# Loading a 1 KB row as 16 transfers of 15 down to 1 and 8 chunks, and another as one transfer of 128 chunks

## The chip, the cores and the metric

The kernel runs on one core of a Trainium2 chip. The metric is the device time of one execution in microseconds (us). Three executions of the kernel before took 666.84, 666.91 and 667.05 us; the median is 666.91 us.

## What is computed

Two decode attention blocks, A and B, with inputs of the same shapes, are computed one after the other and their outputs are put side by side. Each has one token x of 512 numbers, 32 heads of width 128, and a cache of 8192 keys and values for each head. All inputs are bf16. Cut to what matters, one block is:

```python
q = (x @ wq).reshape(B, Sq, H, Dh).transpose(0, 2, 1, 3)        # x: 1 x 1 x 512
scores = einsum("bhqd,bhkd->bhqk", q, k_cache) * (Dh ** -0.5)   # k_cache: 1 x 32 x 8192 x 128
p = softmax(scores, axis=-1)
o = einsum("bhqk,bhkd->bhqd", p, v_cache)
out = o.transpose(0, 2, 1, 3).reshape(B, Sq, H * Dh) @ wo
```

x is 1 KB in each block; the four caches are 64 MB each, and the four weight matrices 4 MB each.

## The kernel before

**Tiling.** The 64 heads of A and B are handled four at a time, in 16 rounds, the "quads". A quad's keys and its values are 8 MB each, laid out over 128 partitions with 32 partitions for each head and 256 positions in each partition, so that a partition holds 64 KB of either. Keys have two buffers (`kn`, two slots used in turn), values have one (`vn`).

**One quad.** VectorE multiplies the keys by the broadcast query in four pieces (`plan_mul`, L338), TensorE sums the products over the width with an identity matrix (`plan_red`, L347), VectorE finishes the sums (L358), the maxima and exponentials follow, and TensorE multiplies the probabilities with the values (`plan_pv`, L416). The value product of a quad is done a round later, between the steps of the next quad.

**Start.** The two query weight matrices are loaded into the buffer of the values (`load_wq`, L281), and x of A and of B into the first partition of the second slot of the keys (`xrow`, L193). TensorE spreads each x over the partitions with four matrix products against ones (`xmm`, L298), reading every fourth number of x at a time, since number m·4+c of x belongs to partition m and piece c. ScalarE copies the result to `xb` (L302). Then `plan_q` makes the queries (L316) and ScalarE copies them out (`qbc`, L324). Queries of A are made at the start and those of B inside the first round, between TensorE's third and fourth reduction of the first quad.

**The order of the transfers.** Every transfer is issued by SyncE (SP) through one helper, `dma` (L243), so all of them show that line; the tiles tell them apart. SP's list is in program order: the query weights of A (`load_wq(0)`, L291), x of A, x of B (L292), the keys of the first quad (`load_k(0)`, L497), the query weights of B (`load_wq(1)`, L498), the keys of the second quad, the values of the first quad, and so on in turn. The first five wait for nothing and are issued before the block of all engines starts (L565). The keys of the second quad overwrite the place where x landed, so `load_k` (L271) has them wait for `x_ready`, the second copy of L302. The values of the first quad overwrite the query weights, so `load_v` (L275) has them wait for `q_done[1]`, the last product with the weights of B. Later keys wait for the reduction that read their slot, later values for the value product before. At the end come the output weights (`load_wo`, L284) in pieces, and the last products with them, a 2 KB output and its transfer.

Of the kernel before, what the change touches and what calls it, by code (L numbers as in the profile page):

```python
# [11 lines left out]
P = 128  # L12
# [11 lines left out]
class _Plan:  # L24
# [15 lines left out]
    def op(self, eng, fn, ctr=None, needs=(), inc=1):  # L40

        for m in needs:
            self.wait(eng, m)
        self.prog[eng].append((fn, ctr, inc))
        if ctr is None:
            return None
        ctr.n += inc
        return ctr, ctr.n
# [81 lines left out]
def bass_concat_heads__mha_block_cached__gqa_block_cached__decode_kernel(  # L130
# [13 lines left out]
    xs = [A_x, B_x]  # L144
# [4 lines left out]
    NA = 2  # L149
    H, Sk, Dh = ks[0].shape[1:]  # L150
    D = xs[0].shape[2]
    NOUT = wos[0].shape[1]
    assert Dh == P and H == 32 and D == 512 and NOUT == 512
    C = D // P
# [19 lines left out]
    with ExitStack() as st:  # L174
        ec = st.enter_context

        def sb(name, shape, dt):
            return ec(nc.sbuf_tensor(name, shape, dt))

        kn = sb("kn", [P, NK, T, Dh], BF16)  # L180
        vn = sb("vn", [P, T, Dh], BF16)

        def flat(ap):
            return ap.rearrange("p t d -> p (t d)")
# [5 lines left out]
        KX, KW = 1, (NM - 2) % NK  # L190
        wo_sb = [flat(kn[:, KW])[:, a * W:(a + 1) * W].rearrange("p (j n) -> p j n", n=NOUT)
                 for a in range(NA)]
        xrow = flat(kn[0:1, KX])[:, 0:NA * D].rearrange("p (a d) -> p a d", a=NA)  # L193
        xb = sb("xb", [P, NA, C, P], BF16)
        qbc = sb("qbc", [P, NM, Dh], BF16)
        pt = sb("pt", [P, T, G], BF16)
# [1 line left out]
        ones_bf = sb("ones_bf", [P, P], BF16)  # L198
# [31 lines left out]
        def ctr(name):  # L230
            return _Ctr(nc, st, name)

        s_x = ctr("s_x")
# [8 lines left out]
        def dma(eng, dst, src, c, needs=()):  # L242
            return op(eng, lambda e: e.dma_start(dst, src), c, needs, inc=16)  # L243
# [37 lines left out]
        def load_wq(a):  # L281
            wq_in[a] = dma("SP", wq_buf[a], wqs[a].rearrange("(p c) n -> p (c n)", p=P), s_w[a])
# [6 lines left out]


        load_wq(0)  # L291
        x_in = [dma("SP", xrow[0:1, a, :], xs[a][0], s_x) for a in range(NA)][-1]  # L292

        for a in range(NA):
            def xmm(e, a=a):
                r = None
                for c in range(C):
                    r = e.matmul((misc if a == 0 else qyp)[:, c * P:(c + 1) * P],  # L298
                                 xrow[0:1, a, c:D:C], ones_bf[0:1, :], start=True, stop=True)
                return r  # L300
            m = op("PE", xmm, c_pe, [x_in, i_onesb])
            x_ready = op("ACT", lambda e, a=a: e.copy(  # L302
                xb[:, a].rearrange("p c m -> p (c m)"), (misc if a == 0 else qyp)[:]), c_act, [m])
# [190 lines left out]
        cuts = {n: [] for n in range(L0, L1 + 1)}  # L494
# [151 lines left out]
```

## Time and profile before

| what | value |
|---|---|
| median of three executions | 666.91 us |
| the profiled execution's own time | 666.67 us |
| its span, first to last instruction | 665.4 us |
| TensorE busy | 437.9 us (66%) |
| VectorE busy | 340.1 us (51%) |
| ScalarE busy | 62.4 us (9%) |
| bytes moved | 285.33 MB in 6076 packets |

The span is what the trace covers; the execution's own time is 1.27 us longer, and what lies outside the span is not shown. Busy times are shares of the span. "PE" is TensorE, "PEld" its loading of weights, "DVE" VectorE, "ACT" ScalarE, "SPq" the sequencer of SyncE that issues transfers. In the lists of instructions each line has a start and a length in us, then engine, line of the code, operation and tiles, how often, and in brackets the idle time before it and what ended it. The lines on transfers give packets, bytes and the share of 16 DMA engines that the packets took; where a short stretch is asked for, a packet counts at its start, so that shares above 100% are possible there.

### The profile page before, as it was taken

Reading aid. Unit: us, or ns where it says so; the run is one execution under the profiler, and the core shown is the slowest. Engines: PE = TensorE matmul, PEld = TensorE weight load, DVE = VectorE, ACT = ScalarE, POOL = GpSimd, SP = SyncE. Lnnn points to the kernel's source line nnn. Section 1 sums busy time; section 2 is a strip of 40 time slices with the busy share of each in tenths; the row PEclk is TensorE's granted clock in tenths of the full one; section 3 lists DMA queues with packets and bytes.
Section 4 is the critical chain, followed back from the end, with each engine's and each line's share of the span. In section 5 each row is a group of like instructions: output and inputs, shape, how many; then the busy total and the mean of one; then the engine's idle time right before and its main releaser. Section 6 shows DMA issues by size and latency. Waiting matters only on the chain.

```text
span 665.4 us, 12448 instructions
## 1 busy us (share of the span) xinstructions
PE 437.9 (66%) x5646; PEld 252.7 (38%) x5646; DVE 340.1 (51%) x215; ACT 62.4 (9%) x151; POOL 2.8 (0%) x15
## 2 busy tenths in 40 slices
PE   1164876938388594838759483875948387594865
PEld 0022342616145261614526161442626144262645
DVE  1094908466390736639083563808356381835610
ACT  1002002020200102020110202010020201002020
POOL 1000000000000000000000000000000000000000
PEclk9998857768786676879667687966768787776875
DMA  9999999999999999999999999999999999999997
GB/s 378 439 443 438 438 432 433 414 433 441 429 433 441 441 437 406 437 441 437 425 441 441 433 410 437 441 437 429 437 441 433 414 433 441 437 429 437 410 440 306
DMA packets 6076, 285.33 MB, mean 429 GB/s; under 512 B 690, under 2 KB 948, under 8 KB 1204
## 3 DMA queue, kind: packets, MB, share of 16 engines
q1 hardware_dynamic: 6068, 285.22, 99.3%
q8 instruction: 6, 0.10, 0.1%
q14 instruction: 2, 0.02, 0.0%
HBM read 285.21 MB, written 0.00 MB: 429 GB/s over the span
## 4 chain that ended last, share of the span: by engine, by line
DMA 63%; PE 25%; DVE 10%; issue 2%; SPq 1%; ACT 0%; DVEq 0%
DMA kn<-in_B_k_cache_dram 27%; DMA kn<-in_A_k_cache_dram 18%; PE rps L347 15%; DMA vn<-in_A_v_cache_dram 14%; DVE kn L338 9%; PE acc L416 9%; DMA kn<-in_B_wo_dram 4%; SPq L243 1%; PE qyp L316 0%; DVE s_sb L358 0%; PE misc L400 0%; ACT qbc L324 0%; DVEq L338 0%; PE bmp L486 0%; PE qyp L474 0%
## 5 line engine op out<-in xcount | busy, mean ns | idle before, releaser
L347 PE MATMUL rps<-kn,ident 128*128 128x512 bf16 x1024 | 290.1, 451 | 169.1 <-DVE kn L338 169.1
L338 DVE TENSOR_TENSOR kn<-kn,qbc 128x8192 bf16<-128x8192 bf16 x64 | 281.5, 4419 | 98.2 <-DMA kn<-in_A_k_cache_dram 58.6
L347 PEld LDWEIGHTS rps<-kn,ident 128*128 128x128 bf16 x1024 | 111.5, 113 | 334.7 <-issue 258.0
L416 PE MATMUL acc<-pt,vn 128*128 128x4 bf16 x4096 | 109.4, 166 | 10.8 <-DMA vn<-in_B_v_cache_dram 5.2
L416 PEld LDWEIGHTS acc<-pt,vn 128*128 128x128 bf16 x4096 | 108.5, 101 | 11.6 <-DMA vn<-in_B_v_cache_dram 5.4
L358 DVE TENSOR_REDUCE s_sb<-rps 128x64 f32<-128x512 f32 x64 | 44.0, 687 | 107.4 <-PE rps L347 107.4
L395 ACT ACTIVATE pt<-s_sb,negb 32x256 bf16<-32x256 f32 x64 | 54.8, 857 | 1.9
L387 ACT ACTIVATE negb<-bmp 128x1 f32<-128x1 f32 x16 | 2.7, 171 | 528.8 <-PE bmp L383 528.8
L425 DVE TENSOR_TENSOR oD<-acc,rinv 128x4 f32 (+1 forms) x16 | 2.6, 162 | 97.2 <-PE acc L416 85.1
L383 PE MATMUL bmp<-gm,hrow 1*128 1x1 f32 x128 | 17.8, 256 | 6.0 <-DVE gm L373 6.0
L383 PEld LDWEIGHTS bmp<-gm,hrow 1*128 1x128 f32 x128 | 16.5, 197 | 10.7 <-DVE gm L373 10.0
L370 PE MATMUL mtp<-ident_f,m 128*1 128x128 f32 x32 | 6.1, 271 | 19.8 <-DVE m L364 19.8
L395 ACT ACTIVATION_READ_ACCUMULATOR pt<-s_sb,negb 32x1 f32 x64 | 15.9, 248 | 0.0
L370 PEld LDWEIGHTS mtp<-ident_f,m 128*1 128x1 f32 x32 | 1.4, 81 | 27.7 <-DVE m L364 27.7
L474 PE MATMUL qyp<-o,kn 128*128 128x1 bf16 x248 | 7.1, 165 | 3.5 <-issue 2.0
L298 PE MATMUL misc<-ones_bf,kn 1*128 1x128 bf16 x4 | 0.6, 302 | 12.9 <-DMA kn<-in_B_x_dram 12.9
L474 PEld LDWEIGHTS qyp<-o,kn 128*128 128x128 bf16 x248 | 6.9, 103 | 3.8 <-issue 2.1
L373 DVE TENSOR_REDUCE gm<-mtp 1x4 f32<-1x128 f32 x16 | 4.5, 279 | 7.5 <-PE mtp L370 7.5
L400 PEld LDWEIGHTS misc<-rsum,ones_f 128*128 128x128 f32 x32 | 6.2, 198 | 3.5 <-issue 1.4
L316 PE MATMUL qyp<-vn,xb 128*32 128x512 bf16 x64 | 6.0, 505 | 2.2 <-ACT qbc L324 1.5
L364 DVE TENSOR_REDUCE m<-s_sb 128x1 f32<-128x256 f32 x16 | 6.7, 420 | 0.5
L324 ACT CAST qbc<-qyp 128x512 bf16<-128x512 f32 x4 | 2.3, 586 | 37.3 <-PE qyp L316 37.3
(36 smaller groups left out, 25.0 us busy)
## 6 DMA issues: line engine op xcount, KB each, us to landing
vn<-in_B_v_cache_dram SPq DMA_DIRECT2D x1, 6144.0 KB, 22.4
vn<-in_A_wq_dram SPq DMA_DIRECT2D x1, 4096.0 KB, 12.3
vn<-in_B_wq_dram SPq DMA_DIRECT2D x1, 4096.0 KB, 39.9
kn<-in_A_wo_dram SPq DMA_DIRECT2D x1, 4096.0 KB, 35.9
kn<-in_B_wo_dram SPq DMA_DIRECT2D x1, 2048.0 KB, 40.5
vn<-in_B_v_cache_dram SPq DMA_DIRECT2D x1, 2048.0 KB, 26.8
kn<-in_B_wo_dram SPq DMA_DIRECT2D x1, 1024.0 KB, 28.8
kn<-in_B_wo_dram SPq DMA_DIRECT2D x1, 512.0 KB, 29.6
```

Source lines behind the costliest of these rows:

```text
L243: return op(eng, lambda e: e.dma_start(dst, src), c, needs, inc=16)
L316: r = e.matmul(qyp[hh * HP:(hh + 1) * HP, :].rearrange("p (i d) -> p i d", d=Dh), xb[:, a, c, hh * HP:(hh + 1) * HP], w, start=(c == 0), s ...
L338: mul_done[n, c] = op("DVE", lambda e: e.tensor_tensor(k, k, qbc[:, nth(n), :].broadcast_to([P, CT, Dh]), ALU.mult), c_mul, [k_in[n], qbc_ ...
L347: r = e.matmul(rps[:, c % 2, :].rearrange("p (t d) -> p t d", d=DW), ident[:], kn[:, i0, c * CT:(c + 1) * CT, i * DW:(i + 1) * DW], start= ...
L358: sr_done[n, c] = op("DVE", lambda e: e.tensor_reduce(s_sb[:, c * CT:(c + 1) * CT], rps[:, c % 2, :].rearrange("p (t d) -> p t d", d=DW), ...
L364: m_done[n] = op("DVE", lambda e: e.tensor_reduce(m1[:], s_sb[:], AX.X, ALU.max), c_dve, [sr_done[n, NCH - 1]])
L370: m = op("PE", lambda e: e.matmul(mtp[0:1, 0:P], m1[:], ident_f[:], start=True, stop=True), c_pe, [m_done[n], i_identf, gm_done.get(n - 1)])
L383: r = e.matmul(bmp[:, 0:1], hrow[0:1, h, :], gm[0:1, h:h + 1], start=(h == 0), stop=(h == G - 1))
L395: p_done[n] = op("ACT", lambda e, h=h, q=q: e.activation(pt[q, :, h], s_sb[q, :], AF.Exp, bias=negb[q, n:n + 1], scale=scale, accum_out=rs ...
L400: m = op("PE", lambda e: e.matmul(misc[:, 0:G], ones_f[:], rsum[:], start=True, stop=True), c_pe, [p_done[n], misc_free[0]])
L416: r = e.matmul(acc[:, 0:G], vn[:, t, :], pt[:, t, :], start=(t == 0), stop=(t == T - 1))
L474: r = e.matmul(qyp[:, i:i + 1], wo_sb[a][:, j, i * P:(i + 1) * P], (o2 if n > 1 else oD)[:, a, j:j + 1], start=(j == 0 and i == 0), stop=( ...
```

## The change

x of A and of B are brought in as chunks of four numbers (8 bytes). In the landing place the chunks no longer touch: each takes the first half of 16 bytes, so that both rows together take 4 KB of the first partition in place of 2 KB. x of A is issued as 16 transfers with 15, 14, 13 and so on down to 1 chunk, and a last one with 8 chunks (128 in all); x of B as one transfer with 128 chunks. All of them count on the same semaphore as before, and the first matrix product waits for all of them together. TensorE now reads x with a step of 16 bytes in place of 8. All else, and the order of all other transfers, stays; SP's list grows by 15 transfers, which stand behind the query weights of A and ahead of the keys of the first quad.

```diff
-        xrow = flat(kn[0:1, KX])[:, 0:NA * D].rearrange("p (a d) -> p a d", a=NA)
+        XCUTS = [tuple(range(15, 0, -1)) + (8,), (P,)]
+        assert all(sum(cuts) == P for cuts in XCUTS)
+        xrow = flat(kn[0:1, KX])[:, 0:2 * NA * D].rearrange("p (a m e) -> p a m e", a=NA, e=2 * C)
...
         load_wq(0)
-        x_in = [dma("SP", xrow[0:1, a, :], xs[a][0], s_x) for a in range(NA)][-1]
+        for a in range(NA):
+            i = 0
+            for n in XCUTS[a]:
+                x_in = dma("SP", xrow[0:1, a, i:i + n, 0:C],
+                           xs[a][0].rearrange("o (m c) -> o m c", c=C)[:, i:i + n, :], s_x)
+                i += n
...
                 for c in range(C):
                     r = e.matmul((misc if a == 0 else qyp)[:, c * P:(c + 1) * P],
-                                 xrow[0:1, a, c:D:C], ones_bf[0:1, :], start=True, stop=True)
+                                 xrow[0:1, a, :, c], ones_bf[0:1, :], start=True, stop=True)
```

## The prediction, made before the run

> **What bounds the kernel now.** I read the page's slices first, then the queues, then the chain that ended last, then the list of SP's transfers at the start.
>
> ```profile
> span 665.4 us, 12448 instructions
> PE 437.9 (66%) x5646; PEld 252.7 (38%) x5646; DVE 340.1 (51%) x215; ACT 62.4 (9%) x151; POOL 2.8 (0%) x15
> DMA  9999999999999999999999999999999999999997
> DMA packets 6076, 285.33 MB, mean 429 GB/s; under 512 B 690, under 2 KB 948, under 8 KB 1204
> q1 hardware_dynamic: 6068, 285.22, 99.3%
> DMA 63%; PE 25%; DVE 10%; issue 2%; SPq 1%; ACT 0%; DVEq 0%
> ```
>
> The DMA engines are at nine tenths or more in every slice but the last, and one queue's packets fill 99.3% of 16 engines' span. No other engine comes near: TensorE is at 66%. So the span is the time to the first packet, plus the packets one behind the other, plus a short tail. The shares of the chain (DMA 63%, PE 25%) don't contradict it: where the chain runs over PE, transfers were under way beside it. Asked for the stretch from 1.7 to 662.7 us alone, the queue stands at 99.9%:
>
> ```profile
> q1 hardware_dynamic: 6052, 285.22, 99.9%
> ```
>
> Two things follow. Nothing that only speeds or delays another engine counts unless it lets the queue run dry. And time that the DMA engines spend on more packets, or wait for an issue, goes to the end nearly whole: there is no later gap in which to make it up, 0.1% of 661 us being 0.7 us.
>
> **Where the change stands.** The start of SP's list, and who waits there:
>
> ```profile
> 0.80 0.38 SPq L243 DMA_DIRECT2D vn<-in_A_wq_dram  x1
> 1.23 0.32 SPq L243 DMA_DIRECT2D kn<-in_A_x_dram  x1
> 1.61 0.23 SPq L243 DMA_DIRECT2D kn<-in_B_x_dram  x1
> 1.88 0.36 SPq L243 DMA_DIRECT2D kn<-in_A_k_cache_dram  x1
> 2.28 0.52 SPq L243 DMA_DIRECT2D vn<-in_B_wq_dram  x1
> 14.61 0.33 SPq L243 DMA_DIRECT2D kn<-in_A_k_cache_dram  x1
> 53.60 0.33 SPq L243 DMA_DIRECT2D vn<-in_A_v_cache_dram  x1
> ...
> 12.86 0.61 PE L298 MATMUL misc<-ones_bf,kn 1*128 1x128 bf16 x4 [12.86 <-DMA kn<-in_B_x_dram]
> ...
> 19.32 0.58 ACT L324 CAST qbc<-qyp 128x512 bf16<-128x512 f32 x1 [2.08 <-PE qyp L316]
> ...
> 32.48 8.76 DVE L338 TENSOR_TENSOR kn<-kn,qbc 128x8192 bf16<-128x8192 bf16 x2 [28.70 <-DMA kn<-in_A_k_cache_dram]
> ```
>
> x is issued at 1.23 and 1.61 us but lands only near 12.8, since it stands behind 4 MB of weights. So SP is some ten microseconds ahead of the DMA engines; that lead is the cover of this change. How much of it there is, two short stretches tell. In the first (0 to 2 us, 40 slices of 0.05 us) the packets of the weights begin in the 37th slice, at 1.80 us, which is 1.0 us behind their issue at 0.80. In the second (12.0 to 12.9, slices of 0.0225 us) 36 packets start: 16 completions of the weights, x (two packets of 1 KB and two completions) and the first 16 packets of the first keys, which stand out by their size, from the 10th slice (12.20) to the 36th (12.79).
>
> ```profile
> GB/s 0 0 0 0 0 0 0 0 0 0 0 0 0 0 0 0 0 0 0 0 0 0 0 0 0 0 0 0 0 0 0 0 0 0 0 0 1966 655 1966 1311
> ...
> GB/s 0 0 0 0 46 0 46 0 0 8738 2913 2913 0 0 0 0 2913 2913 2913 5826 2913 5826 0 0 5825 0 0 0 0 0 0 0 0 0 0 2913 0 0 0 0
> DMA packets 36, 1.05 MB, mean 1167 GB/s; under 512 B 18, under 2 KB 20, under 8 KB 20
> ```
>
> So the 16 engines go over to the keys between 12.20 and 12.79 us, and an issue that is to have packets there must start 1.0 us ahead: by 11.2 us for the first engine and 11.8 for the last. Now it starts at 1.88. The lead is 9.3 to 9.9 us.
>
> **Part 1: 15 more issues on SP.** Seventeen transfers stand where two stood; with d for the issue of one and 0.05 us between two (1.23 + 0.32 to 1.61 is 0.06, 1.61 + 0.23 to 1.88 is 0.04), the keys are issued at 1.23 + 17·(d + 0.05). No transfer of before scatters chunks, so d isn't in the trace. Bounds from the rows: 0.23 (x of B, the shortest), 0.52 (the weights of B, the longest); between them the six pieces of output weights, which stand back to back like the new ones:
>
> ```profile
> L243 SPq DMA_DIRECT2D kn<-in_B_wo_dram x6: 432/432/433, 598.0 to 633.5; - x6
> ```
>
> I take 0.50, near the upper end: small transfers were issued fast (0.23, 0.32), but these were single runs of bytes, and a pattern of chunks can hardly be simpler for the sequencer. Then the keys are issued at 1.23 + 17·0.55 = 10.6 us, against 11.2: hidden, with 0.6 us to spare. At 0.23 it is 6.0, at 0.52 it is 10.9. The cover is gone where 17·(d + 0.05) reaches 10.0, at d = 0.54, close above the bound; this is the first rival. With the shortest row the lead stays 5 us and nothing is gained by it, because the engines were busy either way.
>
> **Part 2: more packets.** The trace shows how a transfer becomes packets. There are 948 − 690 = 258 packets between 512 B and 2 KB; 256 of them are the two last output weights (128 partitions of 1 KB each), the other two are x: one run, one packet. The output, 8 rows of 256 B, makes 16 packets, which I read as 8 of data and 8 completions:
>
> ```profile
> DMA packets 16, 0.00 MB, mean 2 GB/s; under 512 B 16, under 2 KB 16, under 8 KB 16
> q1 hardware_dynamic: 16, 0.00, 1.2%
> ...
> DMA packets 132, 0.12 MB, mean 138 GB/s; under 512 B 18, under 2 KB 125, under 8 KB 132
> q1 hardware_dynamic: 132, 0.12, 39.4%
> ```
>
> So I count for A 128 data packets and 128 completions (n chunks, n engines), for B 128 and 16: 400, where 4 were. The first pair of rows is a stretch of 1.0 us: 1.2% of 16 us over 16 packets is 12 ns each. The second pair is 0.9 us of mostly 1 KB packets: 39.4% of 14.4 us over 132 is 43 ns. The new packets carry 8 bytes, so 12 ns is nearest; 43 is the upper bound, zero the lower. 396 more packets at 12 ns are 4.75 us of engine time, 0.30 us for each of 16 engines if they spread; at 43 ns, 1.06. If nothing spreads, one engine has 4.7 us more. I take 0.3.
>
> The Trainium skill (DMA: Bandwidth & Descriptors, "Why a DMA increments its semaphore by 16 and not by 1") says that a transfer runs on the largest number of engines up to 16 that divides the slowest dimension of both sides, the lowest-numbered ones first. By this the first engine would get 16 data packets of A with 16 completions and 9 of B, 41 in all, the last engine 9: at 12 ns 0.5 and 0.1 us, in place of 0.3 for all. The two packets of x and the 16 of the output agree with it.
>
> The same page ("Specifications") asks for at least 512 B, since below it the engine reads, modifies and writes. It speaks against 8-byte chunks; if it doubled each data packet of the 256, the sum would be 0.5 us in place of 0.3. The output's 12 ns packets show no such penalty, but whether 8 bytes have it no run here shows.
>
> **Part 3: x later.** x lands behind the last engine's weights and its own packets: 12.86 becomes about 13.7. The queries of A are ready at 19.90 (19.32 + 0.58) and the product that needs them starts at 32.48, so 12.6 us are free. The second keys, waiting for x on SP at 14.61, stand in the queue behind the first keys and the weights of B, which land at 2.28 + 39.9 = 42.2; behind them the values wait until 53.60 anyway, for a product that follows the first keys. Cost nothing, up to some 12 us. TensorE's reading with a step of 16 bytes is eight weight loads, four of them these, and lies in the same cover:
>
> ```profile
> vn<-in_B_wq_dram SPq DMA_DIRECT2D x1, 4096.0 KB, 39.9
> ...
> L298 PEld LDWEIGHTS misc<-ones_bf,kn x4: 106/133/143, 12.9 to 13.1; 1*128 1x128 bf16 x4
> ```
>
> **The sum.** +0.3 us from packets, nothing from issues: 666.67 + 0.3 = 667.0 for an execution like the profiled one. That one lies 0.24 us below the median of the runs, 666.91; I put the forecast on the median: **667.2 us**. Its own range is 666.7 to 668.2 (packets at 0 to 43 ns, and 0.2 us of scatter). About 0.2%, 1.3 us, is what a measurement of this kernel can tell from no change.
>
> **The rivals.**
>
> *First, the queue runs dry (slower).* If chunked transfers take SP longer than 0.54 us each, the DMA engines finish the weights and x and stand still until the keys are issued. The place is the time between 12.2 and 13 us; the price is 17 us for each microsecond of d, and all of it goes to the end. With their packets the engines are through with x at about 12.5 (the middle of 12.20 and 12.79) + 0.3 = 12.8; keys issued at 1.23 + 17·(d + 0.05) begin 1.0 later. For d = 0.60 that is 13.28, a gap of 0.5, and +0.8 with the packets, still within 0.2%; for 0.63 it is 13.79 and +1.3, the bound; for 0.70, 14.98, a gap of 2.2 and +2.5 (669.4); for 0.80, 16.68 and +4.2 (671.1). So the rival as I count it begins at d = 0.63, and what lies between 0.54 and there goes to the forecast. For it: the longest row, 0.52, is less than a fifth below, the new pattern has a step more, and each transfer has its own number of engines. Against it: both x rows were the shortest of all. The chance is 0.36.
>
> *Second, the packets pile up on one engine (slower).* If every chunk went to one engine, it would have 4.7 us more, and each large transfer ends with its slowest engine: up to +4.7, 671.6. Against it stands the output, whose 16 packets in 0.07 us (slices 19 to 21 of 0.025 us) can't all come from one engine one after another at 12 ns. Chance 0.03.
>
> *Third, the change doesn't do what it says.* If the chunks were joined again into few packets, only the issues would remain: 666.9. Chance 0.03, within 0.2%.
>
> *Fourth, faster.* The last engine reaches the end later than the first, and a start spread another way could even them out. The stretch in which the last small packets run, 39.4% busy over 0.9 us, shows that 0.5 us at the very most is lost there: 666.4. More than 0.2% would need the packets themselves to be faster; nothing says so. Chance 0.03 for over 0.2%.
>
> **How the numbers follow.** Forecast 0.55, first rival 0.36, second 0.03, third 0.03, fourth 0.03. The first rival is over 0.2% wherever I count it. Slower 0.39, same 0.58, faster 0.03. The range is to hold 8 in 10: from 666.6 it reaches up into the first rival to d of about 0.75 (670.3), which leaves out some 0.1 above and the faster cases below.
>
> **What would show it.** In the profile after: 17 short issues between 1.2 and 11 us, with d read straight off; the first keys issued at about 10.6; packets 6472, of them 1088 under 512 B; the DMA engines without a gap around 12.8; the first matrix product near 13.7; the last output weights 0.3 us later. The forecast is wrong if the keys' issue starts later than 11.8 us, and then by that lateness; or if the packets of x take long by themselves, seen as a late start of the keys' packets though the issue was early.

## The result, and the profile after

The changed kernel takes 670.10 us (median of six, 669.94 to 670.49) against 667.03 us for the kernel before (median of six, 666.84 to 667.11). The ratio is 1.0049, with a 95% interval of 1.0038 to 1.006: slower by 3.1 us. That lies in the stated range of 666.6 to 670.3, but only because the range reached up into the first rival; the forecast itself, 667.2, did not come true.

The page of the changed kernel, the lines that answer to those of before:

```profile
span 668.7 us, 12463 instructions
PE 441.2 (66%) x5646; PEld 254.1 (38%) x5646; DVE 340.1 (51%) x215; ACT 62.4 (9%) x151; POOL 2.8 (0%) x15
DMA  8999999999999999999999999999999999999997
DMA packets 6472, 285.33 MB, mean 427 GB/s; under 512 B 1088, under 2 KB 1344, under 8 KB 1600
q1 hardware_dynamic: 6464, 285.22, 98.9%
```

The bytes are the same and the packets are those that were counted ahead, 6472 and 1088. Of the 40 slices only the first fell, from 9 to 8, so the loss is to be looked for in the first 17 us. The timeline of SP there (start, length, engine, line, tiles, how many), with the first matrix product and the first product of VectorE:

```profile
0.80 0.39 SPq L245 DMA_DIRECT2D vn<-in_A_wq_dram  x1
1.25 11.66 SPq L245 DMA_DIRECT2D kn<-in_A_x_dram  x16
12.95 0.56 SPq L245 DMA_DIRECT2D kn<-in_B_x_dram  x1
13.55 0.58 SPq L245 DMA_DIRECT2D kn<-in_A_k_cache_dram  x1
...
15.96 0.64 PE L305 MATMUL misc<-ones_bf,kn 1*128 1x128 bf16 x4 [15.96 <-DMA kn<-in_B_x_dram]
...
35.63 8.76 DVE L345 TENSOR_TENSOR kn<-kn,qbc 128x8192 bf16<-128x8192 bf16 x2 [31.84 <-DMA kn<-in_A_k_cache_dram]
```

The first keys are issued at 13.55 us, where the forecast had 10.6 and put the end of the cover at 11.2 to 11.8. They land 3.15 us later than before (35.63 against 32.48), and that is the loss. What the DMA engines did meanwhile, in two stretches: 11.9 to 14.7 us (slices of 0.07 us), and 14.7 to 15.6 us (slices of 0.0225 us):

```profile
GB/s 0 0 0 1 2 3 2 1 2 3 1 1 2 2 1 0 0 0 0 0 0 0 0 0 0 1 0 0 0 0 0 0 0 0 2 3 3 4 2 1
DMA packets 416, 0.00 MB, mean 1 GB/s; under 512 B 416, under 2 KB 416, under 8 KB 416
q1 hardware_dynamic: 416, 0.00, 7.7%
...
GB/s 0 0 0 8738 5825 0 0 0 0 8738 2913 0 0 0 0 0 2913 0 0 0 5825 0 0 0 2913 5825 0 0 0 0 0 0 0 0 0 2913 0 0 0 0
q1 hardware_dynamic: 16, 1.05, 333.9%
```

In the first stretch only small packets start (400 of x, 16 completions of the weights), and they fill 7.7% of it, 0.2 us on each engine. Packets of the weights that began before 11.9 still run at its start. Then, from the fourth slice of the second stretch (14.77) to its 36th (15.49), come the first 16 packets of the keys, which before started from 12.20 to 12.79. The middle moved from 12.50 to 15.13, by 2.63 us. These packets are also slower: 333.9% of 0.9 us is 3.01 us each. Of the kernel before, in the stretch shown with the prediction, the same line reads

```profile
q1 hardware_dynamic: 36, 1.05, 270.4%
```

which is 38.9 us of engine time for the same 16 packets and 20 small ones, 2.4 us each. So a start that is 2.63 us later (0.2 of it the small packets, the rest standing still) and first packets that are 0.6 us slower, called the slow restart below, make the 3.1 us (3.2 by this count).

### The profile page after: what moved, and what is told of

The parts are those of the page before. It is cut to its first block, busy times and chain, and to the rows that moved or that the text cites. A ratio compares the mean times of both kernels' runs of the same rounds, so it can differ in the third digit from the quotient of the medians.

```text
span 668.7 us, 12463 instructions
## 1 busy us (share of the span) xinstructions
PE 441.2 (66%) x5646; PEld 254.1 (38%) x5646; DVE 340.1 (51%) x215; ACT 62.4 (9%) x151; POOL 2.8 (0%) x15
## 2 busy tenths in 40 slices
DMA packets 6472, 285.33 MB, mean 427 GB/s; under 512 B 1088, under 2 KB 1344, under 8 KB 1600
## 4 chain that ended last, share of the span: by engine, by line
DMA 64%; PE 23%; DVE 8%; SPq 2%; issue 2%; ACT 0%; DVEq 0%
DMA kn<-in_A_k_cache_dram 21%; DMA kn<-in_B_k_cache_dram 21%; PE rps L354 13%; PE acc L423 10%; DMA vn<-in_B_v_cache_dram 9%; DMA vn<-in_A_v_cache_dram 9%; DVE kn L345 8%; DMA kn<-in_B_wo_dram 4%; SPq L245 2%; DMA kn<-in_B_x_dram 0%; ACT xb L309 0%; DVE s_sb L365 0%; PE misc L407 0%; PE misc L305 0%; DVEq L345 0%
## 5 line engine op out<-in xcount | busy, mean ns | idle before, releaser
L354 PEld LDWEIGHTS rps<-kn,ident 128*128 128x128 bf16 x1024 | 111.9, 113 | 333.9 <-issue 258.6
```

The costliest lines, as they stand in the source:

```text
L354: r = e.matmul(rps[:, c % 2, :].rearrange("p (t d) -> p t d", d=DW), ident[:], kn[:, i0, c * CT:(c + 1) * CT, i * DW:(i + 1) * DW], start= ...
```

## The experiments

Each time is the median of its kernel; the difference is against the kernel before in the same comparison (666.9 to 667.0 us), with the ratio's 95% interval.

**Issue by ScalarE.** In the changed kernel, the transfers of x go to another sequencer:

```diff
-                x_in = dma("SP", xrow[0:1, a, i:i + n, 0:C],
+                x_in = dma("ACT", xrow[0:1, a, i:i + n, 0:C],
```

> The same 17 chunked transfers of x, with the same packets, are issued by ScalarE's sequencer in place of SP's. Theory 1, the dry queue: SP issues the first keys at about 1.3 us, the DMA engines go from the weights to the keys without a gap, and about 667.2 us are left (the packets alone cost 0.1 to 0.3). Theory 2, the 400 small packets themselves or the disorder they bring to the 16 engines cost the 3 us: about 670. Theory 3, x lands too late: it lands no earlier than 14 us, so about 670 or more.

Measured: 679.22 us, 1.0189 [1.0176, 1.0203], 12 us slower than before. No theory gave this time: the first two are off by 9 us and more, and the third named 670 as a lower bound, for an x that lands from 14 us on. SP's list shows that the keys' lateness is gone and what took its place; the queues' packets between 17 and 41 us show why:

```profile
1.25 0.42 SPq L245 DMA_DIRECT2D kn<-in_A_k_cache_dram  x1
...
46.05 0.33 SPq L245 DMA_DIRECT2D kn<-in_A_k_cache_dram  x1
71.18 0.33 SPq L245 DMA_DIRECT2D vn<-in_A_v_cache_dram  x1
...
44.27 0.64 PE L305 MATMUL misc<-ones_bf,kn 1*128 1x128 bf16 x4 [44.27 <-DMA kn<-in_B_x_dram]
...
q1 hardware_dynamic: 238, 10.42, 100.7%
q10 hardware_dynamic: 202, 0.00, 0.5%
```

x now stands in a second queue (q10), and in 24 us the engines served 202 packets of it and 238 of SP's: about one small packet for each large one of 32 or 64 KB. So the small packets are drawn out over the whole time in which SP's queue has work; 90 of the 400 are still left at 41 us, and the product that reads x starts at 44.27. The Trainium skill (DMA: Bandwidth & Descriptors, "Queues, rings and completion order") states that an engine takes turns between its queues packet by packet; the two counts agree. The second keys wait for x and are issued at 46.05, past the 42 us to which the queue reached: here late x does cost, as Part 3 of the prediction said it would from some 12 us on. The values, which wait for a product behind the first keys, then come late in their turn (71.18 against 53.60). In the 32 us from 42 to 74 SP's packets fill 72.4%, so that about 8.8 us of the 12 are lost there. Of the changed kernel's 3.1 us this run says nothing, since a new wait came in.

**Two transfers of 128 chunks.** `XCUTS = [(P,), (P,)]`, all else as changed.

> x of A as one transfer of 128 chunks like x of B: 2 issues, 288 packets in place of 400. Theory 1: the keys are issued at about 2.5 us, no gap, 667.1. Theory 2, price by packet: 284 of 396 added packets, so 0.72 of 3.1 us, 669.2.

Measured: 668.97 us, 1.0028 [1.0017, 1.004]. The keys are issued at 2.64 us, so nothing runs dry, and yet 2.0 us are lost. Theory 1 alone falls; packets that meet a full queue have a price of their own. Theory 2, a price for each packet, came near with its 669.2; the twelve transfers below speak against it.

**Touching chunks.** The same 17 cuts, each one run of bytes:

```diff
-        xrow = flat(kn[0:1, KX])[:, 0:2 * NA * D].rearrange("p (a m e) -> p a m e", a=NA, e=2 * C)
+        xflat = flat(kn[0:1, KX])[:, 0:NA * D]
+        xrow = xflat.rearrange("p (a m e) -> p a m e", a=NA, e=C)
...
-                x_in = dma("SP", xrow[0:1, a, i:i + n, 0:C],
-                           xs[a][0].rearrange("o (m c) -> o m c", c=C)[:, i:i + n, :], s_x)
+                x_in = dma("SP", xflat[0:1, a * D + i * C:a * D + (i + n) * C],
+                           xs[a][0][:, i * C:(i + n) * C], s_x)
```

> The same 17 cuts, but the chunks touch in the landing place as they do at the source, so that each transfer is one run of bytes. If the number of transfers made SP late, the keys are again issued near 13.5 us and the time is 670. If the pattern of chunks did (my theory), each issue takes 0.23 to 0.33 us as x did before, the keys are issued at 6 to 8 us, no gap: 667.0.

Measured: 667.47 us, 1.0007 [0.9998, 1.0016]. The issues of the 16 transfers of x of A in this kernel and, below, in the changed one (minimum, median, maximum in ns):

```profile
L246 SPq DMA_DIRECT2D kn<-in_A_x_dram x16: 228/252/323, 1.2 to 5.8; - x16
```

```profile
L245 SPq DMA_DIRECT2D kn<-in_A_x_dram x16: 419/690/956, 1.2 to 12.2; - x16
```

So SP is late by the pattern of chunks, not by the number of transfers alone: 0.25 us for a run, 0.69 for chunks in one partition.

**Twelve transfers.** `XCUTS = [tuple(range(15, 4, -1)) + (18,), (P,)]`.

> x of A as 12 chunked transfers (15 down to 5 chunks, and one of 18), nearly the same packets (391 in place of 400). Theory 1: by the issue times of the changed kernel the first keys are issued near 11.3 us, the edge of the cover, so 667.1 to 667.6. Theory 2: 0.98 of the loss remains, 670.0.

Measured: 668.36 us, 1.002 [1.0011, 1.0029]: between the two expectations. The issue of the first keys, and the packets from 12 to 15 us (slices of 0.075 us; numbers near 875 and its multiples are packets of 64 KB):

```profile
11.13 0.59 SPq L245 DMA_DIRECT2D kn<-in_A_k_cache_dram  x1
...
GB/s 0 0 0 3 4 1753 880 2626 1 877 877 876 0 0 0 874 874 874 1 874 1748 0 0 0 874 0 0 0 0 0 0 0 0 0 0 0 0 0 0 0
q1 hardware_dynamic: 423, 1.05, 115.3%
```

By the prediction's bound the keys come in time (11.13 against 11.2), and 1.4 us are lost all the same, with nearly the same packets as in the changed kernel. Two things are seen. The 16 first packets of the keys start from 12.4 to 13.8, where they took from 12.20 to 12.79 before. And they are slow: 115.3% of 3 us on 16 engines is 55.3 us, and less 3.4 us for 407 small packets (8 ns each, as 7.7% of 2.8 us gave for 416) 3.2 us are left for each, as after a stop. So this run lies on the edge of the cover. How its 1.4 us divide between keys that come a little late and packets that get in the way of others, it can't tell. The next five runs look for the price of the packets where the keys are issued long ahead.

**Extra packets beside the kernel before.** To the kernel before, with its own x, two transfers are added that nobody reads. In the first form, ahead of L292:

```diff
+        for a in range(NA):
+            dst = flat(kn[0:1, KX])[:, 4096 + a * 1024:5120 + a * 1024].rearrange("p (m e) -> p m e", e=8)[:, :, 0:4]
+            src = xs[a][0].rearrange("o (m c) -> o m c", c=4)
+            dma("SP", dst, src, s_x)
```

> The kernel before with x loaded as before, and ahead of it two more transfers of 128 chunks of 8 bytes, from x into unused room of the same partition, 16 bytes apart (288 packets more; nothing reads them). It measures the packets alone beside transfers that are already queued. Theory R (an engine that meets many small packets in a row loses its lead in reading, whatever they touch): 669.0, as the version with two chunked transfers. Theory P (the writes to one partition collide): 669.0. Theory S (the reads of the same 2 KB collide): 669.0. My prediction's 12 ns a packet: 667.2.

Measured: 668.98 us, 1.0031 [1.0019, 1.0042], +2.0 us. With `dst = kn[:, KX, 32 + a, 0:4]`, a partition for each chunk:

> The same two extra transfers, but each of the 128 chunks goes to a partition of its own. Theory R: 669.0. Theory P: 667.2. Theory S: 669.0.

Measured: 668.41 us, 1.002 [1.0011, 1.0029], +1.4 us. With `src = ks[a][0, 0:1].rearrange("o (m r) d -> o m r d", r=64)[:, :, 0, 0:4]` and one partition:

> The same two extra transfers into one partition, but the chunks are read 16 KB apart from the key cache. Theory R: 669.0. Theory P: 669.0. Theory S: 667.2.

Measured: 667.84 us, 1.0013 [1.0004, 1.0022], +0.8 us. With `e=64`, `c=32` and `0:32` in place of `0:4` in the first form, that is 16 chunks of 64 bytes:

> The two extra transfers as 16 chunks of 64 bytes each, one packet and one completion for an engine and transfer (64 packets in place of 288). Theory R: 667.1 to 667.5, since each engine meets two data packets and not 16. A price by packet: 64 of 288, 667.4. A fixed price for each chunked transfer: 669.0.

Measured: 666.92 us, 1.0 [0.9991, 1.0009]: nothing. No single theory fits: spreading the reads saves more than half of the 2.0 us, spreading the writes above a quarter (this second saving is within the intervals, which overlap). So both were spread:

> The kernel before with two extra transfers of 128 chunks of 8 bytes that are read 16 KB apart and written to 128 partitions. If the two collisions, of reads in one 2 KB and of writes in one partition, are all that small packets cost, 667.0. If an engine also loses its lead in reading by their number, the first packets of the keys are still longer than 2.42 us and 667.4 to 667.8 are left.

Measured: 667.02 us, 1.0001 [0.9992, 1.001]: nothing is left of the price, although there are as many packets of 8 bytes as in the first form. Theory R falls, P and S hold together. The bytes moved between 12 and 15 us (slices of 0.075 us as before) show it, first with both in one place, then with both spread:

```profile
GB/s 1 0 2 1 3 2 16 876 1 15 1749 1 875 1 1 1 1 875 874 875 0 1 874 0 1748 0 1748 0 874 0 0 0 0 0 874 874 874 0 0 0
```

```profile
GB/s 0 0 3 1752 1753 3514 891 2622 0 1 4 2623 875 0 0 0 0 0 0 0 0 0 0 0 0 0 0 0 0 0 0 0 0 0 0 874 2621 3495 874 2621
```

In the first the first packets of the keys straggle from the 8th slice to the 37th, 2.2 us apart; in the second the 16 engines are all at the keys by the 13th slice, and the second packets begin at the end of the row. There the price is engines held up behind their small packets while others already stream. With the reads spread and the writes in one partition, the same stretch reads

```profile
GB/s 0 1 875 15 17 2626 2626 1753 2624 876 1750 875 0 0 0 0 0 0 0 0 0 0 0 0 0 0 0 0 0 0 0 0 0 0 0 0 0 0 0 0
q1 hardware_dynamic: 324, 1.05, 105.4%
```

All 16 start by the 12th slice, as early as with both spread, but 105.4% of 48 us, less 2.6 us for 308 small packets, is 3.0 us for each in place of 2.4. So here the 0.8 us are slow first packets, though the keys were issued long before (3.38 us) and no stop came ahead of them.

**The dry queue by itself.** In the kernel before, the first keys wait for x as the second do; there are no chunks anywhere:

```diff
-                          [x_ready if n == KX else red_done.get((n - NK, NCH - 1))])
+                          [x_ready if n <= KX else red_done.get((n - NK, NCH - 1))])
```

> The kernel before, with x loaded as before, but the first keys wait on SP for x_ready, so that they are issued at about 14.6 us with no small packet anywhere. The dry queue by itself. If a dry queue goes to the end in full: first packets of the keys at about 15.7 in place of 12.4, +3.2, and if the first packets after a stop take about 0.6 us longer as they did in the changed kernel, +3.8: 670.8 (670.2 without that). If the small packets made the loss: 667.

Measured: 670.94 us, 1.006 [1.0046, 1.0073], +4.0 us. SP's issue, the packets between 13 and 15.8 us, and those from 15.8 to 16.8 us:

```profile
14.84 0.36 SPq L243 DMA_DIRECT2D kn<-in_A_k_cache_dram  x1
...
DMA packets 0, 0.00 MB, mean 0 GB/s; under 512 B 0, under 2 KB 0, under 8 KB 0
...
q1 hardware_dynamic: 16, 1.05, 309.9%
```

Not one packet in 2.8 us, then 16 of 3.10 us each. A stop goes to the end, with some 0.7 us of slow restart on top, and here chunks have no part in either.

**More transfers.** `XCUTS = [tuple(range(14, 0, -1)) + (8, 3, 4, 4, 4), (P,)]`: 19 for A, the same 400 packets.

> The changed kernel with x of A in 19 transfers in place of 16 (14 down to 1, then 8, 3, 4, 4, 4 chunks), the same 400 packets. Dry queue: the keys are issued 2 us later, near 15.5, and the time is 672.0. A price by packet or by chunk: 670.1, as the changed kernel.

Measured: 671.96 us, 1.0075 [1.0062, 1.0089], as the dry queue has it:

```profile
15.33 0.58 SPq L245 DMA_DIRECT2D kn<-in_A_k_cache_dram  x1
```

1.78 us later than in the changed kernel, for 2.0 us more against the kernel before.

**Sixteen times eight chunks.** `XCUTS = [(8,) * 16, (P,)]`.

> The changed kernel with x of A in 16 transfers of 8 chunks each, the same number of transfers and packets. If an issue of any chunked pattern takes about 0.65 us, the keys are issued near 13.1 and the time is 669.7. If it was the counts that aren't powers of two that made SP slow, an issue takes 0.56 or less, the keys are issued by 12.0 and the time is 668.5.

Measured: 669.35 us, 1.0036 [1.0022, 1.0049], nearer to the first. The interval leaves room for the second too; the length of an issue decides:

```profile
12.65 0.58 SPq L245 DMA_DIRECT2D kn<-in_A_k_cache_dram  x1
...
L245 SPq DMA_DIRECT2D kn<-in_A_x_dram x16: 620/620/792, 1.2 to 11.4; - x16
```

An issue of eight chunks takes 0.62 us, so the uneven counts made it only some 0.07 us worse; the chunked pattern is the bulk.

Side by side, by the issue of the first keys:

| kernel | first keys issued, us | against before, us |
|---|---|---|
| two extra transfers, both spread | 2.84 | +0.1 |
| two chunked transfers | 2.64 | +2.0 |
| twelve transfers | 11.13 | +1.4 |
| sixteen of eight chunks | 12.65 | +2.4 |
| the changed kernel | 13.55 | +3.1 |
| keys wait for x, no chunks | 14.84 | +4.0 |
| nineteen transfers | 15.33 | +5.1 |

From 12.65 to 15.33, over three chunked kernels, the issue comes 2.68 us later and the time grows by 2.6 us (671.96 against 669.35). At 2.64 the queue doesn't run dry, and what is left is the packets in each other's way. The row at 11.13 lies between the two.

## Why the prediction was wrong, and where it was right

*What bounds the kernel* held: a queue that is always full leaves no place to make time up, and 3.15 us of later landing at the start came out as 3.1 at the end. The bounds of the cover, 11.2 to 11.8 us, were a little late: they rest on 1.0 us from an issue to its first packet, and behind chunked transfers it took 1.2 (13.55 to 14.77), which makes them 11.0 to 11.6. The run with the keys at 11.13 stands just past the first of these and had slow first packets already.

*Part 1* is the step that failed. It took 0.50 us for an issue and capped it with 0.52, the longest row of a trace in which no transfer had a chunked pattern in one partition. Measured, 17 issues fill 1.25 to 13.55 us, so d is 12.30 / 17 − 0.05 = 0.67. The text gave 0.54 as the point where the cover ends and 0.63 as the point where it shows, so the mechanism stood there, as the rival; what was held against it were x's own fast issues (0.23 and 0.32), which were runs of bytes and say nothing of chunks, as the touching chunks show.

*The first rival's price* was too low. With d = 0.67 its formula gives the keys' packets at 14.5, a gap of 1.7 and +2.0 us. It took 1.0 us from issue to packets, but behind a chunked transfer the keys' own issue grew from 0.36 to 0.58, and the middle of the packets came 1.58 us behind it. And it had no term for the restart, 0.6 us. So it was partly luck that the range held: its upper end was worked out for d = 0.75, and for the measured d the rival's formula gives 668.9, 1.2 us below what was measured.

*Part 2* had the count right to the packet and the price wrong in its nature. As the time of a packet itself, 12 ns was near (8 ns in the changed kernel); but what a packet costs is what it holds up. 288 small packets (256 of 8 bytes and 32 completions) cost nothing where reads and writes are spread, and 2.0 us where all are read from the two rows of 1 KB and are written to the same partition beside a running stream. In the changed kernel that price hardly shows: the small packets run while the queue is empty behind them, the keys' first packets start within 0.7 us of each other, and the gap and the restart already account for 3.2 us. The 512 bytes of the Trainium skill (DMA: Bandwidth & Descriptors, "Specifications"), below which a transfer is not at line rate and the engine reads, modifies and writes, were weighed in the prediction as a price for each packet; 288 small packets at +0.1 us, inside the interval, do not show one.

*Part 3* held for the changed kernel in its cost, though not in its time: the first product with x started at 15.96 (forecast 13.7), as late as its issue made it, and nothing waited for it that wasn't waiting for the keys. The run with ScalarE shows where it ends.

*The second rival*, all chunks on one engine, doesn't fit the count of 128 completions for A, if an engine posts one for its share of a transfer. Touching chunks do go as one packet with one completion for each transfer: the page of that kernel has 6106 packets, 30 more than before for 15 more transfers. On which engine, the views don't show.

What stays open: what makes the reads, and the writes, of small packets get in each other's way; why the first large packets are slow, after a stop and also beside writes to one partition; how the 1.4 us of the twelve transfers divide; and the 0.5 us of the touching chunks, whose interval just reaches no change.

## What to carry to other kernels

Where transfers bound a kernel, the issuing sequencer's lead is a budget in microseconds: add up the issues that stand ahead of the next large transfer and compare with the time at which the queue empties, less the time from issue to first packet, and leave a margin: at the very edge the first packets were slow already. A row for one form of transfer is no bound for another form. In these runs small packets were nearly free when they neither read nor wrote one place, and they did not belong in a second queue beside large ones where somebody waited for them.

## What the runs showed of the hardware that was not expected

- The issue of a transfer depends on its pattern: 0.25 us for a run of bytes, 0.62 for eight chunks in one partition, up to 0.96 for the first of the changed kernel with 15; the transfer behind a chunked one is slower too (0.58 against 0.36). 128 chunks into 128 partitions took 0.42:

```profile
L243 SPq DMA_DIRECT2D kn<-in_B_k_cache_dram x1: 424/424/424, 1.7 to 1.7; - x1
```

- After a stop the first packet of 64 KB on each engine took 3.0 us (changed kernel) and 3.1 us (keys wait for x) in place of 2.4. The same length was seen without a stop, 3.0 us, behind small packets that write one partition.
- Two queues on the same engines took turns, 202 small packets to 238 of the other queue in 24 us, so a transfer of 8-byte packets issued by 13.5 us was ready for its reader only at 44 us.
- 288 small packets cost 2.0 us with reads and writes each in one place, 1.4 with only the writes spread, 0.8 with only the reads spread, and nothing measurable with both spread.
